# The g vector as a per-partition factor on the transposed q, and weight sums in four units

## The chip, the cores and the metric

The kernel runs on one core of a Trainium2 chip. A core has five engines that work side by side, each through its own queue in order: TensorE (PE, matrix products), VectorE (DVE), ScalarE (ACT), GpSimd (POOL) and SyncE (SP, which here only issues transfers). The metric is the time of one execution on the device in microseconds (us); the median of several runs counts.

## What is computed

Attention over 8 batches and 12 heads (448 rows, 64 columns) with root-mean-square norms on q and k, and then two matrix products with a leaky ReLU between them. Cut to what matters:

```python
def rmsnorm(x, g):
    rms = np.sqrt(np.mean(x * x, axis=-1, keepdims=True) + 1e-06)
    return x / rms * g
q_n, k_n = rmsnorm(q, g_q), rmsnorm(k, g_k)
scores = (1.0 / np.sqrt(64)) * np.matmul(q_n, k_n.transpose(0, 1, 3, 2))
attn = np.exp(scores - np.max(scores, axis=-1, keepdims=True))
attn = attn / (np.sum(attn, axis=-1, keepdims=True) + 1e-09)
o = np.matmul(attn, v)                      # (8, 12, 448, 64)
x = o.transpose(0, 2, 1, 3).reshape(3584, 768)
h = x @ w_in                                # (3584, 2048)
out = np.maximum(0.01 * h, h) @ w_out       # (3584, 768)
```

g_q, g_k and the factor 1/8 enter the scores only as the product 0.125 * g_q[d] * g_k[d] for each of the 64 columns d. The kernel applies that product to q alone.

## The kernel before

**Units.** A unit u is four heads of one batch: 24 units, three for each batch. The raw q and k of a unit lie in tiles `rq` and `rk` with 128 rows of tokens on the partitions, and 2 x 7 x 64 numbers on each. A ring of three such pairs is loaded four units ahead by SP (L107).

**Preparing a unit.** The squares `sq` are made on ACT (`prep_sq`, L130) or on POOL (`prep_sqp`, L134). DVE sums them (`ssq`, L143), ACT makes `rinv` from the sums by a logarithm and an exponential (L148, L149), and DVE multiplies raw q and raw k by it into `n16`, or n (L155, one instruction for q and one for k, 896 numbers a partition). n is then transposed into `qkT`, in which partition 64a + d holds column d of head half a. Units 0 to 5 do this on PE, with a copy out of PSUM on DVE or ACT (`prep_tr`, L163 and L164). Units 6 to 23 use a transposing DMA that SP issues (`prep_trd`, L167).

**The g product before the change.** At the start, g_q and g_k come as two rows on one partition (`grow`, L564 and L565, issued by ACT). DVE multiplies them (L573), a PE product with a column of ones spreads the row over all 128 partitions (L574), and ACT copies it to `ggb` (L578). For each unit POOL multiplies raw q in place by `ggb` (`prep_qg`, L138). This happens after the squares were taken from raw q and ahead of n.

**A unit's attention.** Scores are made in seven steps of PE (L183) into PSUM, with keys on the partitions. ACT takes their exponentials (`et`, L202), shifted by a bound that is taken from step 0: DVE reduces the scores to a maximum (`shift_max`, L220) and spreads it on a diagonal matrix dg (L222), PE multiplies it with ones (`shift_mm`, L232), DVE reduces again (L233) and forms the bias (L241). In PE's queue `shift_mm` stands behind the PV product (L324) and the column sums (`zc`, L270) of the unit before; everything later on PE stands behind it. The column sums are inverted on DVE and ACT (L287 to L293), spread by DMA (`rz`, L297), and POOL multiplies the PV result with them (`xmul_pool`, L304, writing `xt`).

**The two matrix products.** They are cut into items, in a queue. Each unit has four stages d = 0 to 3, and `fill` pops items between the attention work, in shares laid down in `WD`; after each item it runs one of the small jobs of that stage, and what is left of them at the stage's end. So the order on every engine is fixed when the program is built. Items are `moe1` (the first product, six matmuls of L345 and the leaky ReLU on ACT, L339), `moe2` (the plain second product, L385), and `seven` (the second product of two tiles by seven products of half-size blocks instead of eight, L425). `seven` needs sums of blocks of the activations (`s1`, `s2` on DVE, L406 and L409; `s3`, `s4` on POOL, L412 and L415) and four sums of blocks of `w_out` (`tw`, L400). The latter are made once, each in two halves of 1536 numbers a partition, on DVE: two sums in stage 3 of unit 5, two in stage 3 of unit 6. The first `seven` comes after the 16 `moe1` items of batch 1, which are queued in stage 3 of unit 6.

**Order in a steady unit u (u > 3).** Stage 0: scores, `shift_max`, PV and sums of u-1, `shift_mm`, exponentials; the load of u+4, `prep_qg` of u+2 and the v load of u+3 on POOL. Stage 1: `xmul_pool` of u-1, `ssq` of u+2. Stage 2: `rinv`, n and the transpose of u+2. Stage 3: weight sums, where there are any, and the squares of u+3 on ACT from unit 6 on.

Of the kernel before, what the change touches and what calls it, by code (L numbers as in the profile page):

```python
# [8 lines left out]
FP32 = mybir.dt.float32  # L9
FP16 = mybir.dt.float16  # L10
AF = mybir.ActivationFunctionType
ALU = mybir.AluOpType
# [6 lines left out]
def kernel(  # L19
# [11 lines left out]
    nc = tc.nc  # L31
# [4 lines left out]
    P = 128  # L36
# [18 lines left out]
    def aux(shape, dtype, name):  # L55
        return psum.tile(shape, dtype, tag="aux", bufs=4, name=name)
# [10 lines left out]
    nc.vector.memset(onesp, 1.0)  # L67
    eps_t = cst.tile([P, 1], FP32)
    nc.vector.memset(eps_t, 1.0e-6)
    one32 = cst.tile([1, P], FP32)  # L70
    nc.vector.memset(one32, 1.0)
    grow = cst.tile([1, 2, D], FP32)
    gate_t = cst.tile([P, 1], FP16)
    ggb = cst.tile([P, D], FP32)
    vts = [cst.tile([P, 2, NS, D], FP16, name=f"vt{i}") for i in range(NV)]
    win16 = cst.tile([P, NQ, 2, DF], FP16)
    wout16 = cst.tile([P, FT, DM], FP16)
# [42 lines left out]
    def buf(u, name):  # L120
        if name not in st[u]:
            shape, dtype, bufs = SHAPES[name]
            st[u][name] = prep_p.tile(shape, dtype, tag=name[:2] if bufs == 3 and name != "qkT" else name, bufs=bufs, name=name)
        return st[u][name]
# [8 lines left out]
        for ti in tis:  # L133
            nc.gpsimd.tensor_tensor(buf(u, f"sq{ti}"), raw[u][ti], raw[u][ti], op=ALU.mult)  # L134

    def prep_qg(u, eng, c=ALL):
        n = c[1] - c[0]
        eng.tensor_tensor(raw[u][0][:, :, c[0]:c[1]], raw[u][0][:, :, c[0]:c[1]],  # L138
                          ggb[:, None, None, :].broadcast_to([P, 2, n, D]), op=ALU.mult)

    def prep_ssq(u, c=ALL, tis=BOTH):
        for ti in tis:
# [16 lines left out]
    def prep_tr(u, ti, copies):  # L159
        tp = aux([P, NS, P], FP16, "tp")  # L160
        for (lo, hi), copy in copies:
            for x in range(lo, hi):
                nc.tensor.transpose(tp[:, x, :], buf(u, "n16")[:, ti, x].rearrange("p a d -> p (a d)"), ident16)  # L163
            copy(buf(u, "qkT")[:, ti, lo:hi], tp[:, lo:hi])  # L164

    def prep_trd(u):
        nc.sync.dma_start_transpose(  # L167
# [383 lines left out]
            job()  # L551
        flush()

    vcopy, acopy = nc.vector.tensor_copy, nc.scalar.copy
    CA, CB = (0, 4), (4, NS)
    K0, K1 = (0, 1), (1, NS)
    VV = ((ALL, vcopy),)
# [1 line left out]
    def warm(n, bank):  # L559
        for x in range(n):  # L560
            nc.tensor.matmul(bank[:, P:2 * P], onesp, onesp, start=True, stop=True)

    with tc.manual_schedule():
        nc.scalar.dma_start(grow[:, 0], g_q[None, :])  # L564
        nc.scalar.dma_start(grow[:, 1], g_k[None, :])  # L565
        nc.scalar.preload_act_table_set("natural_log_exp_and_others")
        load(0)
        load(1)
        load(2)
        gps = aux([P, 512], FP32, "gps")  # L570
        wbank = aux([P, 512], FP32, "warm")
        warm(32, wbank)
        nc.vector.scalar_tensor_tensor(grow[:, 0], grow[:, 0], 0.125, grow[:, 1], op0=ALU.mult, op1=ALU.mult)  # L573
        nc.tensor.matmul(gps[:, 0:D], one32, grow[:, 0], start=True, stop=True)  # L574
        warm(42, wbank)
        prep_sq(0, CA, (0,))
        prep_sq(0, CB, (0,))
        acopy(ggb, gps[:, 0:D])  # L578
        prep_sq(0, ALL, (1,))
        prep_qg(0, nc.gpsimd, CA)  # L580
        prep_qg(0, nc.gpsimd, CB)
        prep_ssq(0, CA, (0,))
        prep_ssq(0, CB, (0,))
        prep_rinv(0, (0,))
# [22 lines left out]
        prep_sq(2, ALL, (0,))  # L607
        load(3)
        gate(0)
        prep_qg(1, nc.gpsimd)  # L610
        prep_sqp(2, (1,))
        shift_max(0)
        shift_bank(0)
# [5 lines left out]
        def feed(u):  # L619
            load(u + 4)  # L620
            gate(u + 1)
            prep_qg(u + 2, nc.gpsimd)
            prep_sqp(u + 3)
            load_v(u + 3)

# [113 lines left out]
        for u in range(3, NU):  # L739
            for d in range(4):  # L740
# [18 lines left out]
                def job(fn, *args):  # L759
                    jobs.append(lambda: fn(*args))  # L760

                if d == 0:
                    if u == 3:
                        prep_norm(4)
                        gate(4)
                    elif narrow(u - 1):
                        job(zcol_inv, u - 1)
                    else:
                        xmul(u - 1)
                    if u + 4 < NU:  # L770
                        job(load, u + 4)
                    if u + 2 < NU:
                        prep_qg(u + 2, nc.gpsimd)
                    if u + 3 < NU:
                        load_v(u + 3)
                    if u < 6:
                        prep_sqp(u + 3)
# [4 lines left out]
                if (u, d) in ((3, 1), (4, 0)):  # L782
                    for ti in range(2):
                        prep_tr(u + 1, ti, VV)
                if u + 2 < NU:
                    if d == 1:
                        for ti in range(2):
                            job(prep_ssq, u + 2, ALL, (ti,))
                    if d == 2:
                        job(prep_rinv, u + 2)  # L790
                        for ti in range(2):
                            job(prep_norm, u + 2, ALL, (ti,))
                        if u > 3:
                            job(prep_trd, u + 2)
                if d == 3 and u in (5, 6):
                    for n in (0, 2) if u == 5 else (1, 3):
                        for x in range(2):
                            job(weight_sum, n, x)
                if d == 3 and 6 <= u < NU - 3:
                    for ti in range(2):  # L800
                        job(prep_sq, u + 3, ALL, (ti,))
# [37 lines left out]
```

## Time and profile before

| what | value |
|---|---|
| time, median of 5 runs | 444.38 us (443.87, 444.55, 444.38, 442.57, 1426.18) |
| the profiled execution | 442.99 us; its span 441.2 us |
| PE busy | 411.9 us, 93% |
| ACT busy | 309.4 us, 70% |
| DVE busy | 256.4 us, 58% |
| POOL busy | 191.4 us, 43% |
| g pass on POOL (L138), 25 times | 52.4 us, mean 2.098 us |
| xt pass on POOL (L304), 19 times | 40.1 us, mean 2.113 us |
| n on DVE (L155), 25 for q and 25 for k | 31.3 and 29.9 us |
| ssq on DVE (L143), 49 times | 50.2 us, mean 1.053 us |
| weight sums on DVE (L400), 8 times | 0.94 to 2.84 us each |
| transposing DMA (L167), 18 times | 4.1 us from issue to landing |

The span is the time from the first to the last instruction of the profiled execution; the time of an execution is a little longer. Busy shares are averages over the whole span. An engine's idle time counts only where the work that ends last stood behind it. In a listing by time each line has the start, the duration, the engine, the line of the program, the operation with output and input tiles and their shapes, and in brackets how long the engine had been idle and what released it. A group that runs back to back is one line with its count. The page also has a row for the clock that PE was granted, in tenths of full speed, over 40 equal slices of the span.

### The profile page before, as it was taken

What the parts mean: (1) busy time and instruction counts of PE and PEld (TensorE: products, weight loads), DVE (VectorE), ACT (ScalarE), POOL (GpSimd) and SP (SyncE); (2) the same over time, 40 slices, a digit from 0 to 9 for tenths busy, and PEclk for the clock granted to TensorE, in tenths of its full rate; (3) what the DMA queues carried; (4) which work ended last, traced back from release to release, by engine and by line L of the source; (5) the groups of instructions that cost most, each with busy time, mean ns of one, the idle gap of its engine ahead of it and who ended that gap; (6) DMA issues with size and microseconds to landing.
All of it is one profiled execution on the core that took longest, in us unless ns stands there. A gap on an engine that the chain in (4) does not pass through costs nothing.

```text
span 441.2 us, 8892 instructions
## 1 busy us (share of the span) xinstructions
PE 411.9 (93%) x3645; PEld 211.1 (48%) x3645; DVE 256.4 (58%) x381; ACT 309.4 (70%) x470; POOL 191.4 (43%) x132
## 2 busy tenths in 40 slices
PE   7788999677999899999999999999999999999996
PEld 7544444333344444454445444454445544555563
DVE  5897666868365954566476873386377650422062
ACT  6998977455788459977788589976987658653400
POOL 4996752604144641264255732364237601050250
PEclk9999999969799999999999999999999999999999
DMA  8999995846525597657845796748753441112004
GB/s 263 230 258 242 244 242 82 204 78 181 144 45 144 96 227 200 122 129 188 198 87 138 129 226 177 178 84 205 195 69 72 124 114 43 43 37 71 0 8 136
DMA packets 66476, 62.37 MB, mean 141 GB/s; under 512 B 35716, under 2 KB 61572, under 8 KB 66436
## 3 DMA queue, kind: packets, MB, share of 16 engines
q1 hardware_dynamic: 55840, 49.62, 43.7%
q0 software_dynamic: 10272, 11.80, 17.3%
q8 instruction: 28, 0.46, 0.4%
q10 hardware_dynamic: 324, 0.39, 0.3%
q14 instruction: 12, 0.10, 0.1%
HBM read 45.61 MB, written 11.01 MB: 128 GB/s over the span
## 4 chain that ended last, share of the span: by engine, by line
PE 69%; DVE 14%; ACT 11%; issue 5%; DVEq 0%; ACTq 0%
PE hps L345 31%; ACT et L202 7%; PE ma L425 6%; PE sT L183 6%; PE md L425 5%; PE op L385 5%; PE sT L324 4%; DVE n L155 4%; PE mc L425 3%; PE mb L425 3%; PE zc L270 2%; DVE tw L400 2%; DVE sT L220 2%; DVE ost L432 1%; DVE ssq L143 1%
## 5 line engine op out<-in xcount | busy, mean ns | idle before, releaser
L202 ACT ACTIVATE et<-sT,eb 128x896 f16<-128x896 f32 x166 | 158.6, 1005 | 16.6 <-PE sT L183 15.0
L345 PE MATMUL hps<-xt,win 128*128 128x448 f16 x756 | 153.6, 357 | 0.2 <-DVE xt L333 0.2
L345 PEld LDWEIGHTS <-win 128*128 128x128 f16 x756 | 71.4, 99 | 73.4 <-issue 13.2
L304 POOL TENSOR_TENSOR xt<-x,rz 128x896 f16<-128x896 f32 x19 | 40.1, 2113 | 131.8 <-DMA rz<-zs 109.1
L339 ACT ACTIVATE gt<-hps 128x448 f16<-128x448 f32 x126 | 66.0, 541 | 22.1 <-PE hps L345 21.4
L138 POOL TENSOR_TENSOR rq<-rq,ggb 128x896 f32<-128x896 f32 (+2 forms) x25 | 52.4, 2098 | 41.7 <-ACT sq L130 28.5
L155 DVE TENSOR_TENSOR n<-rq,rinv 128x896 f16<-128x896 f32 (+2 forms) x25 | 31.3, 1255 | 59.9 <-issue 42.3
L183 PE MATMUL sT<-qkT 64*64 64x448 f16 x664 | 52.2, 363 | 5.4 <-ACT et L202 4.7
L282 ACT COPY x<-sT 128x896 f32<-128x896 f32 x19 | 17.2, 906 | 50.8 <-DVE sT L233 48.1
L143 DVE TENSOR_REDUCE ssq<-sq 128x14 f32<-128x896 f32 (+2 forms) x49 | 50.2, 1053 | 1.0 <-ACT sq L130 1.0
L425 PEld LDWEIGHTS <-sa 128*128 128x128 f16 x352 | 32.8, 98 | 26.3 <-issue 6.1
L412 POOL TENSOR_TENSOR sa<-gt 128x512 f16<-128x512 f16 (+1 forms) x15 | 25.8, 1721 | 28.4 <-ACT gt L339 24.5
L385 PE MATMUL op<-wout,gt 128*128 128x384 f16 x192 | 36.3, 341 | 0.0
L425 PEld LDWEIGHTS <-gt 128*128 128x128 f16 x264 | 25.2, 98 | 20.6 <-issue 4.6
L220 DVE TENSOR_REDUCE sT<-sT 128x1 f32<-128x896 f32 x22 | 24.0, 1092 | 18.8 <-PE sT L183 18.8
L183 PEld LDWEIGHTS <-qkT 64*64 64x64 f16 x672 | 15.8, 104 | 39.5 <-issue 35.5
L415 POOL TENSOR_TENSOR sa<-gt,sa 128x512 f16<-128x512 f16 (+1 forms) x15 | 26.7, 1777 | 15.1 <-DVE sa L409 10.5
L425 PE MATMUL ma<-wout,gt 128*128 128x384 f16 x176 | 32.3, 326 | 0.1
L155 DVE TENSOR_TENSOR n<-rk,rinv 128x896 f16<-128x896 f32 (+2 forms) x25 | 29.9, 1198 | 0.0
L324 PE MATMUL sT<-et,vt 64*64 64x448 f16 x532 | 28.5, 349 | 0.3
L406 DVE TENSOR_TENSOR sa<-gt 128x512 f16<-128x512 f16 (+1 forms) x15 | 10.7, 710 | 30.3 <-ACT gt L339 30.3
L385 PEld LDWEIGHTS <-gt 128*128 128x128 f16 x192 | 18.4, 102 | 15.5 <-issue 5.7
(86 smaller groups left out, 454.4 us busy)
## 6 DMA issues: line engine op xcount, KB each, us to landing
rq<-in_q_dram SPq DMA_DIRECT2D x24, 448.0 KB, 5.0
rk<-in_k_dram SPq DMA_DIRECT2D x24, 448.0 KB, 6.1
out_dram<-ost SPq DMA_DIRECT2D x52, 192.0 KB, 3.5
rz<-zs SPq DMA_DIRECT2D x38, 224.0 KB, 3.2
vt<-in_v_dram POOLq DMA_DIRECT2D x24, 224.0 KB, 4.4
win<-in_moe_w_in_dram POOLq DMA_DIRECT2D x8, 384.0 KB, 12.2
wout<-in_moe_w_out_dram POOLq DMA_DIRECT2D x2, 1536.0 KB, 28.6
out_dram<-ost SPq DMA_DIRECT2D x4, 96.0 KB, 2.1
```

The costliest lines, as they stand in the source:

```text
L138: eng.tensor_tensor(raw[u][0][:, :, c[0]:c[1]], raw[u][0][:, :, c[0]:c[1]], ggb[:, None, None, :].broadcast_to([P, 2, n, D]), op=ALU.mult)
L143: nc.vector.tensor_reduce(buf(u, "ssq")[:, ti, :, c[0]:c[1]], buf(u, f"sq{ti}")[:, :, c[0]:c[1]], axis=AXL.X, op=ALU.add)
L155: nc.vector.tensor_tensor(buf(u, "n16")[:, ti, c[0]:c[1]].rearrange("p s a d -> p a s d"), src[:, :, c[0]:c[1]], buf(u, "rinv")[:, ti, :, ...
L183: nc.tensor.matmul(banks[a][64 * r:64 * r + 64, 0:S].rearrange("p (t x) -> p t x", t=NS), kT(u, r, a, t), qT(u, r, a), start=True, stop=True)
L202: nc.scalar.activation(s["et"][:, t], sT[:, :, 0:S], AF.Exp, bias=s["eb"], scale=1.0)
L220: nc.vector.tensor_reduce(s["spare"][:, 511:512], sT[:, :, 0:S], axis=AXL.XY, op=ALU.max)
L304: nc.gpsimd.tensor_tensor(xts[b][:, g], s["x32"], s["rz"], op=ALU.mult)
L324: nc.tensor.matmul(s["pv"][r][64 * a:64 * a + 64, 0:S], vts[u % NV][64 * r:64 * r + 64, a, t], s["et"][64 * r:64 * r + 64, t, a], start=(t ...
L339: nc.scalar.activation(dst, src, AF.Prelu, bias=0.0, scale=1.0, alpha=0.01)
L345: nc.tensor.matmul(hps[:, 0:S], win16[:, kt // 2, kt % 2, ts(ft, P)], xt[:, kt // 2, kt % 2], start=(kt == 0), stop=(kt == KT - 1))
L385: nc.tensor.matmul(op2[:, 0:HC], gt[:, ft, ds(col(t), P)], wout16[:, ft, ds(HC * half, HC)], start=(ft == 0), stop=(ft == FT - 1))
L425: nc.tensor.matmul(bank[:, 0:HC], a[:, f], b[:, f], start=(first and f == 0), stop=(f == HF - 1), skip_group_check=not first)
```

## The change

POOL's pass over raw q is gone for all units. The vectors g_q and g_k are loaded with their 64 numbers on 64 partitions, twice (partitions 0 to 63 and 64 to 127), g_q by two DMAs of ACT and g_k by two of POOL. One DVE instruction makes `gcol` = 0.125 * g_q * g_k, one number on each partition. The q half of `qkT` is multiplied by it: in units 0 to 5 inside the copy out of PSUM (on DVE a multiplication in place of a copy, on ACT a copy with a scale), in units 6 to 23 by a DVE instruction of its own, in place on `qkT`, in stage 1 of the unit before (`prep_g`). The row product on PE, its PSUM bank and ACT's copy fall away, and the 74 warming products of PE at the start become 75 in one piece. The weight sums come in stage 3 of units 4, 5, 6 and 7, one sum (two halves) in each, instead of two sums in unit 5 and two in unit 6. The order of the four sums is now 0, 1, 2, 3; it was 0, 2, 1, 3.

```diff
@@ -67,11 +67,9 @@
     nc.vector.memset(onesp, 1.0)
     eps_t = cst.tile([P, 1], FP32)
     nc.vector.memset(eps_t, 1.0e-6)
-    one32 = cst.tile([1, P], FP32)
-    nc.vector.memset(one32, 1.0)
-    grow = cst.tile([1, 2, D], FP32)
+    gpair = cst.tile([P, 2], FP32)
+    gcol = cst.tile([P, 1], FP32)
     gate_t = cst.tile([P, 1], FP16)
-    ggb = cst.tile([P, D], FP32)
     vts = [cst.tile([P, 2, NS, D], FP16, name=f"vt{i}") for i in range(NV)]
     win16 = cst.tile([P, NQ, 2, DF], FP16)
     wout16 = cst.tile([P, FT, DM], FP16)
@@ -133,10 +131,8 @@
         for ti in tis:
             nc.gpsimd.tensor_tensor(buf(u, f"sq{ti}"), raw[u][ti], raw[u][ti], op=ALU.mult)
 
-    def prep_qg(u, eng, c=ALL):
-        n = c[1] - c[0]
-        eng.tensor_tensor(raw[u][0][:, :, c[0]:c[1]], raw[u][0][:, :, c[0]:c[1]],
-                          ggb[:, None, None, :].broadcast_to([P, 2, n, D]), op=ALU.mult)
+    def prep_g(u):
+        nc.vector.tensor_scalar(buf(u, "qkT")[:, 0], buf(u, "qkT")[:, 0], gcol, None, op0=ALU.mult)
 
     def prep_ssq(u, c=ALL, tis=BOTH):
         for ti in tis:
@@ -161,7 +157,7 @@
         for (lo, hi), copy in copies:
             for x in range(lo, hi):
                 nc.tensor.transpose(tp[:, x, :], buf(u, "n16")[:, ti, x].rearrange("p a d -> p (a d)"), ident16)
-            copy(buf(u, "qkT")[:, ti, lo:hi], tp[:, lo:hi])
+            copy(buf(u, "qkT")[:, ti, lo:hi], tp[:, lo:hi], ti == 0)
 
     def prep_trd(u):
         nc.sync.dma_start_transpose(
@@ -551,7 +547,18 @@
             job()
         flush()
 
-    vcopy, acopy = nc.vector.tensor_copy, nc.scalar.copy
+    def vcopy(dst, src, scaled=False):
+        if scaled:
+            nc.vector.tensor_scalar(dst, src, gcol, None, op0=ALU.mult)
+        else:
+            nc.vector.tensor_copy(dst, src)
+
+    def acopy(dst, src, scaled=False):
+        if scaled:
+            nc.scalar.activation(dst, src, AF.Copy, bias=0.0, scale=gcol)
+        else:
+            nc.scalar.copy(dst, src)
+
     CA, CB = (0, 4), (4, NS)
     K0, K1 = (0, 1), (1, NS)
     VV = ((ALL, vcopy),)
@@ -561,24 +568,19 @@
             nc.tensor.matmul(bank[:, P:2 * P], onesp, onesp, start=True, stop=True)
 
     with tc.manual_schedule():
-        nc.scalar.dma_start(grow[:, 0], g_q[None, :])
-        nc.scalar.dma_start(grow[:, 1], g_k[None, :])
+        for a in range(2):
+            nc.scalar.dma_start(gpair[64 * a:64 * a + 64, 0:1], g_q[:, None])
+            nc.gpsimd.dma_start(gpair[64 * a:64 * a + 64, 1:2], g_k[:, None])
         nc.scalar.preload_act_table_set("natural_log_exp_and_others")
         load(0)
         load(1)
         load(2)
-        gps = aux([P, 512], FP32, "gps")
         wbank = aux([P, 512], FP32, "warm")
-        warm(32, wbank)
-        nc.vector.scalar_tensor_tensor(grow[:, 0], grow[:, 0], 0.125, grow[:, 1], op0=ALU.mult, op1=ALU.mult)
-        nc.tensor.matmul(gps[:, 0:D], one32, grow[:, 0], start=True, stop=True)
-        warm(42, wbank)
+        warm(75, wbank)
+        nc.vector.scalar_tensor_tensor(gcol, gpair[:, 0:1], 0.125, gpair[:, 1:2], op0=ALU.mult, op1=ALU.mult)
         prep_sq(0, CA, (0,))
         prep_sq(0, CB, (0,))
-        acopy(ggb, gps[:, 0:D])
         prep_sq(0, ALL, (1,))
-        prep_qg(0, nc.gpsimd, CA)
-        prep_qg(0, nc.gpsimd, CB)
         prep_ssq(0, CA, (0,))
         prep_ssq(0, CB, (0,))
         prep_rinv(0, (0,))
@@ -607,7 +609,6 @@
         prep_sq(2, ALL, (0,))
         load(3)
         gate(0)
-        prep_qg(1, nc.gpsimd)
         prep_sqp(2, (1,))
         shift_max(0)
         shift_bank(0)
@@ -619,7 +620,6 @@
         def feed(u):
             load(u + 4)
             gate(u + 1)
-            prep_qg(u + 2, nc.gpsimd)
             prep_sqp(u + 3)
             load_v(u + 3)
 
@@ -769,8 +769,6 @@
                         xmul(u - 1)
                     if u + 4 < NU:
                         job(load, u + 4)
-                    if u + 2 < NU:
-                        prep_qg(u + 2, nc.gpsimd)
                     if u + 3 < NU:
                         load_v(u + 3)
                     if u < 6:
@@ -782,6 +780,8 @@
                 if (u, d) in ((3, 1), (4, 0)):
                     for ti in range(2):
                         prep_tr(u + 1, ti, VV)
+                if d == 1 and 5 <= u < NU - 1:
+                    job(prep_g, u + 1)
                 if u + 2 < NU:
                     if d == 1:
                         for ti in range(2):
@@ -792,10 +792,9 @@
                             job(prep_norm, u + 2, ALL, (ti,))
                         if u > 3:
                             job(prep_trd, u + 2)
-                if d == 3 and u in (5, 6):
-                    for n in (0, 2) if u == 5 else (1, 3):
-                        for x in range(2):
-                            job(weight_sum, n, x)
+                if d == 3 and 4 <= u < 8:
+                    for x in range(2):
+                        job(weight_sum, u - 4, x)
                 if d == 3 and 6 <= u < NU - 3:
                     for ti in range(2):
                         job(prep_sq, u + 3, ALL, (ti,))
```

## The prediction

> **What bounds the kernel now.** I read the page first (engine shares, clock row, chain), then the list of TensorE's waits, then the timeline of the stretches where those waits lie, and last the clock in slices of 1 us there. TensorE (PE) is busy 412 of 441 us, and the chain of waits is 69% PE. ACT has the second highest share (309 us), but over 164 to 180 us PE is busy 16.0 of 16.0 us with ACT at 14.3. So a change pays only where PE stands still, or runs slowly. The page's clock row and chain, and PE's waits:
>
> ```profile
> PEclk9999999969799999999999999999999999999999
> PE 69%; DVE 14%; ACT 11%; issue 5%; DVEq 0%; ACTq 0%
> ...
> PE sT L232 <- DVE dg L222: 12.7, 5, 6.1
> ```
>
> The clock row has two dips, slices 8 and 10 (88 to 99 and 110 to 121 us). The wait line says that in five places PE stood for 12.7 us in all, 6.1 in the longest, for the small matrix dg that VectorE (DVE) makes when a unit's score maximum is known. PE's timeline gives the three that count; the bracket is the idle time ahead of the instruction:
>
> ```profile
> 91.10 0.27 PE L232 MATMUL sT<-dg,onesp 128*128 128x64 f16 x2 [6.07 <-DVE dg L222]
> ...
> 110.82 0.26 PE L232 MATMUL sT<-dg,onesp 128*128 128x64 f16 x2 [3.78 <-DVE dg L222]
> ...
> 148.00 0.22 PE L232 MATMUL sT<-dg,onesp 128*128 128x64 f16 x2 [2.16 <-DVE dg L222]
> ```
>
> Why is dg late? The timeline of DVE and GpSimd (POOL) ahead of the first (start, duration, engine, line):
>
> ```profile
> 79.91 1.08 DVE L155 TENSOR_TENSOR n<-rq,rinv 128x896 f16<-128x896 f32 x1
> 80.16 2.77 POOL L304 TENSOR_TENSOR xt<-x,rz 128x896 f16<-128x896 f32 x1 [1.69 <-DMA rz<-zs]
> 80.91 2.97 DVE L155 TENSOR_TENSOR n<-rk,rinv 128x896 f16<-128x896 f32 x1
> ...
> 82.89 2.94 POOL L138 TENSOR_TENSOR rq<-rq,ggb 128x896 f32<-128x896 f32 x1
> 83.81 2.83 DVE L400 TENSOR_TENSOR tw<-wout 128x1536 f16<-128x1536 f16 x1
> ...
> 86.57 0.54 DVE L389 COPY ost<-op 128x384 f32<-128x384 f32 x1
> 87.03 2.68 DVE L400 TENSOR_TENSOR tw<-wout 128x1536 f16<-128x1536 f16 x3
> 89.64 1.09 DVE L220 TENSOR_REDUCE sT<-sT 128x1 f32<-128x896 f32 x1
> ```
>
> PE finished unit 5's PV and column sums at 85.03 and stood. DVE had to do n, then four weight sums, then the maximum (L220). The first sum took 2.83 us, the next three 0.89 each: it began while POOL ran the g pass (L138), and ended 0.8 us after it (82.89 + 2.94 = 85.83). The n ahead was held in the same way by POOL's xt.
>
> Ahead of 110.82 it is the same: four sums from 104.00, one of them 2.83 us under the g pass of 106.12. Ahead of 148.00 no sum runs, but L406 (0.69 us elsewhere) took 2.21 under the g pass of 143.51. The stall also has a second price, shown by the clock in slices (columns: PE, PE loads, DVE, ACT, POOL busy, then clock):
>
> ```profile
> 88.00:89.00 1.00, 0.00 (x0) 0.00 (x0) 1.00 (x2) 0.00 (x0) 0.00 (x0) 0.94 0.77 98
> 89.00:90.00 1.00, 0.00 (x0) 0.00 (x0) 1.00 (x2) 0.00 (x0) 0.00 (x0) 0.50 0.72 114
> ...
> 94.00:95.00 1.00, 1.00 (x5) 0.44 (x4) 0.00 (x0) 0.64 (x2) 0.00 (x0) 0.50 0.00 0
> 95.00:96.00 1.00, 1.00 (x5) 0.43 (x3) 0.00 (x0) 0.00 (x0) 0.00 (x0) 0.64 0.03 7
> 96.00:97.00 1.00, 1.00 (x13) 0.42 (x12) 0.79 (x2) 0.47 (x1) 0.00 (x0) 1.00 0.92 197
> ```
>
> The clock is halved from about 89 to 95.6, so that 16 matmuls of L385 take 4.80 us there against 2.71 later. After 110.82, 18 of L345 take 5.99 against 3.51.
>
> **What the Trainium skill says.** "SBUF — State Buffer", section "SBUF: two separate sides": VectorE with two SBUF inputs (or in a two-port mode) and GpSimd share a port pair under an exclusive lock, held for a whole instruction. The trace agrees: 2.83 against 0.89 us. "TensorE: Matmul & The Clock Gate", Part 1: the clock halves after a mostly idle window of about 3.4 us, and the window runs freely. Here it fell 3.9 us after PE stopped at 85.03 and 2.6 after it stopped at 107.04, and not in the stall of 2.16. "VectorE: DVE Perf Modes", the perf-mode tier table: a fp16 tensor_scalar in SBUF runs at four elements a cycle, from PSUM at two at most, like a copy. The trace has no such instruction; its PSUM copy (L164, 0.61 us for 896) fits the two. "DMA: Bandwidth & Descriptors", Anatomy of one DMA: a POOL-issued DMA has some 2.0 us fixed. The g loads here, issued by ACT, took about 2.6 us (end of issue 1.53, DVE's use at 4.16).
>
> **The change part by part.** DVE's hand-over is 1.46 us from the start of L220 to PE's L232 (89.64 to 91.10). "Boundary u" is that of unit u.
>
> *g passes removed.* 25 on POOL, 52.4 us, none itself on PE's path except through the lock. At boundary 9, L406 falls from 2.21 to 0.69: 1.5 us gained, all of it inside a stall of 2.16. POOL's next work there, a v load and the L412 pass, must wait for PE's PV first, so that it shouldn't move into the gap. POOL's earlier squares and loads in the first 44 us free nobody on the chain: n follows DVE's own work or ACT's rinv there.
>
> *Weight sums spread.* Eight pieces of 0.9 us, two at each of boundaries 5 to 8, instead of four at 6 and 7.
> - Boundary 5 (new): DVE was free at 70.21 (0.17 us ahead of L220). 70.21 + 1.8 + 1.46 = 73.5 against PE's 72.29: 1.2 us lost.
> - Boundary 6: sums start at 83.81, no g pass: 0.9 + 0.47 (the ost copy) + 0.9 + 1.46 gives 87.54 against 91.10. Gain 3.56; a stall of 2.5 remains (from 85.03), since xt still holds n.
> - Boundary 7: 104.00 + 1.8 + 1.46 = 107.26 against 110.82. Gain 3.56; 0.2 remains.
> - Boundary 8 (new): L409 ended at 126.73; + 1.8 + 1.46 = 130.0 against 129.19: 0.8 lost. But L415 on POOL (1.15 us) comes free at that moment; as at 80.9, where xt got in between two DVE passes, it will likely hold the second sum. I take 1.9; the ends are 0.8 and 3.0 (held twice).
> - Clock: 5.99 − 3.51 = 2.48 back after boundary 7, surely, since 0.2 us of stall can't halve it. After boundary 6, 4.80 − 2.71 = 2.09 back if 2.5 us of stall keep the clock. That lies between the 2.16 that kept it and the 2.64 that didn't; I take it as kept. The other end is 0.
>
> *g as a factor of qkT.* Units 6 to 23: 18 tensor_scalar on DVE. By the skill's breakdown (150 + 8 + 224 cycles at 0.96 GHz) an estimate of 0.40 us each, 1.1 at one element a cycle. They wait for a transpose issued a unit earlier, landed after 4.1 us, so nothing stands behind them. They lie ahead of the ssq, after which DVE is idle (6.2 us ahead of 174.86; still 2.5 us at 157 in a unit with the seven products). Cost 0 at both ends; without that gap 7.2 us in all. Units 0 to 5: the factor is in the PSUM copies. DVE's at 0.61 as before: 0. At one element a cycle each would take 0.44 more, three of them on the chain of the first 44 us: +1.3.
>
> *Start.* Out: the g row product, its matmul and copy on ACT (0.4 us between the squares), two g passes (2.23 us). n of the second q chunk waited for them. In: four loads of 64 single numbers, two on POOL behind its mask work (1.31), and a product on DVE queued ahead of the first ssq, for which ACT's rinv, n and all of unit 0 wait. Two POOL issues at 0.77 each end at 2.85; 2.0 to 2.6 us later the product runs, at 4.9 to 5.5 instead of 4.16. The first ssq, 4.70 before, starts at 5.1 to 5.7. Reduction of k then ends at 7.3 to 7.9 against 7.59. Gain 0.2, from −1.0 to +0.7.
>
> **Sum.** −1.2 + 3.56 + 3.56 + 2.48 + 2.09 − 1.9 + 1.5 + 0.2 = 10.3 us. The profiled execution took 442.99 us (span 441.2): 432.7. The median of the runs shown is 444.38, 1.4 above it: 434.1 is the forecast.
>
> **The rivals.**
> 1. *The clock still halves at boundary 6* (the window falls badly). Gain 8.2: 436.2. For: 2.64 us sufficed once. Against: 2.16 didn't. 0.25.
> 2. *More falls away*: boundary 8 at 0.8, the start at its best: 12 us, 432.4 and less. 0.12.
> 3. *A new late one eats half*: g lands at 8 us or PSUM copies run at one element a cycle, and something behind boundary 7 comes late (xt is done 9.9 us after L232, its matmuls due at about 9.9 once warm). 438 to 443. 0.04.
> 4. *Slower: four stalls for two.* Place: boundaries 5 to 8. If every piece meets a POOL pass (2.83 each, 3.9 more per boundary), the stalls are 5.1, 6.4, 4.1 and 4.7, each with a cold clock at about 2.3: 29.5 us against today's 6.07 + 3.78 + 2.09 + 2.48 = 14.4. Less 1.7 for boundary 9 and the start, +13.4: 457.8. It decides from about 4 us a boundary with its cold stretch. For: xt, L412 and L415 stay on POOL. Against: the pass that held the sums was the g pass each time, and around 70 and 104 POOL would be empty. 0.08 with all else that ends above.
> 5. *No change* within 0.3% (1.3 us, about what can be told apart here): 0.03.
>
> **How the numbers follow.** Forecast 0.48. Faster: 0.48 + 0.25 + 0.12 + 0.04 = 0.89; same 0.03; slower 0.08. The range 430 to 440 takes in both clock cases, both ends of boundary 8 and of the start, and the slower copies; outside are 4, 5 and the tails of 2 and 3, some 0.15.
>
> **What would show it.** Right: PE's wait for L222 falls from 12.7 to about 7 us; no stall over 3 us; the clock row without its second dip; sums at 0.9 us each; L406 never at 2.2. Wrong: sums of 2.8 us, dips at four places, a first ssq after 6 us, or tensor_scalar rows above 1.1 us.

## The result, and the profile after

The changed kernel takes 442.74 us (median of 44 executions) against 443.80 (79 executions of the kernel before): ratio 0.9967, interval 0.9953 to 0.9981. It is faster, by about 1 us or 0.2 to 0.5%. The forecast was 10 us, and 442.74 lies outside its range of 430 to 440.

The executions of the changed kernel do not lie around one value: 17 lie from 438.9 to 440.5 us, nine from 442.6 to 443.2 and 16 from 444.1 to 444.8. The other two, of 528 and 1352 us, stand apart, and as the one of 1352 us (mean matmul of L341 937 ns instead of 353) was the one profiled, the profile below is of the same kernel in run r1. That execution took 439.96 us and belongs to the first group.

Of its page, the span, the clock row, the chain by engine, and of PE's waits the two longest:

```profile
span 438.1 us, 8869 instructions
...
PEclk9698999989999999999999999999999999999999
...
PE 63%; ACT 17%; DVE 13%; issue 4%; DMA 2%; POOL 0%; DVEq 0%; POOLq 0%; ACTq 0%
...
PE sT L228 <- DVE dg L218: 6.9, 7, 2.5
PE tp L159 <- DVE n L151: 4.7, 1, 4.7
```

The wait for dg fell from 12.7 to 6.9 us, and no single stall is above 2.5 us. But a transfer has come onto the chain (DMA 2%), there is a new wait of 4.7 us for n, and the clock row has dips near its start. The code has moved by some lines: in the changed kernel `shift_mm` is L228, the weight sums are L396, s1 is L402, s3 and s4 are L408 and L411, xt is L300 and n is L151; runs with added lines differ by a few more. PE's timeline shows the boundaries of units 5, 6, 8 and 9 (boundary u is where PE waits for dg of unit u):

```profile
78.92 0.22 PE L228 MATMUL sT<-dg,onesp 128*128 128x64 f16 x2 [0.92 <-DVE dg L218]
94.08 0.22 PE L228 MATMUL sT<-dg,onesp 128*128 128x64 f16 x2 [2.44 <-DVE dg L218]
127.88 0.22 PE L228 MATMUL sT<-dg,onesp 128*128 128x64 f16 x2 [2.46 <-DVE dg L218]
145.31 0.22 PE L228 MATMUL sT<-dg,onesp 128*128 128x64 f16 x2 [0.47 <-DVE dg L218]
```

The forecast had 1.2, 2.5, 1.9 (ends 0.8 and 3.0) and 0.7 here. So the boundaries are about where they were expected, except unit 8, which lies above the 1.9 of the sum. The start is not. Its timeline, over all engines:

```profile
0.74 1.20 ACTq L572 DMA_DIRECT2D gpair<-in_g_q_dram  x2
...
2.34 0.55 POOL L573 DMA_DIRECT2D gpair<-in_g_k_dram  x1
...
2.89 1.48 POOL L108 DMA_DIRECT2D vt<-in_v_dram  x2
...
7.90 0.95 ACT L128 ACTIVATE sq<-rk 128x896 f32<-128x896 f32 x1 [2.65 <-DMA rk<-in_k_dram]
9.84 0.16 DVE L580 SCALAR_TENSOR_TENSOR gcol<-gpair 128x1 f32<-128x1 f32 x1 [8.49 <-DMA gpair<-in_g_k_dram]
9.91 2.13 DVE L139 TENSOR_REDUCE ssq<-sq 128x8 f32<-128x512 f32 x3
...
12.70 0.40 PE L159 MATMUL tp<-ident,n 128*128 128x128 f16 x4 [4.72 <-DVE n L151]
```

DVE stood 8.5 us for g, and the first ssq behind it in its queue started at 9.91 us; before it was 4.70. One column was enough to hold the engine that everything at the start goes through. After PE had stood, its clock was halved, from 13.2 to 20.0 us, and again from 33.7 to 37.1; in the kernel before it was whole until 88.9.

The table splits the spans at the same instructions of PE: the first wait of the first matrix product for DVE's xt ("first product"), `shift_mm` at boundaries 5, 6 and 8, and the first wait of an md product (one of the products of `seven`) for DVE, at 160.82 us before.

| stretch, us | before | changed (r1, 439.96 us) | r6, 444.60 us | r12 |
|---|---|---|---|---|
| start to first product | 43.47 | 49.12 | 48.80 | 44.05 |
| to boundary 5 | 28.82 | 29.80 | 29.81 | 29.81 |
| to boundary 6 | 18.81 | 15.16 | 15.16 | 15.16 |
| to boundary 8 | 38.09 | 33.80 | 33.54 | 33.53 |
| to the md product | 31.63 | 30.18 | 35.35 | 30.33 |
| to the end | 280.38 | 280.04 | 280.14 | 279.92 |
| span | 441.2 | 438.1 | 442.8 | 432.8 |

r6 is the changed kernel with two v loads issued later, which leaves everything after the start as it was. Its profiled execution took 444.60 us, and shows where such executions lose 5 us: in one stretch, from boundary 8 to the md product.

### The profile page after: what moved, and what is told of

It is laid out like the page before. It is cut to its first block, busy times and chain, and to the rows that moved or that the text cites. A ratio compares the mean times of both kernels' runs of the same rounds, so it can differ in the third digit from the quotient of the medians.

```text
span 1349.9 us, 8869 instructions
## 1 busy us (share of the span) xinstructions
PE 1343.1 (99%) x3644; PEld 435.2 (32%) x3644; DVE 255.1 (19%) x398; ACT 325.7 (24%) x469; POOL 137.4 (10%) x109
## 4 chain that ended last, share of the span: by engine, by line
PE 99%; ACT 0%; DVE 0%; issue 0%
PE hps L341 38%; PE sT L179 9%; PE op L381 8%; PE ma L421 7%; PE md L421 7%; PE mc L421 7%; PE sT L320 7%; PE mb L421 4%; PE zc L266 3%; PE pv L320 2%; PE warm L568 2%; PE sT L249 1%; PE tp L159 1%; PE pb L568 1%; PE sT L348 1%; PE zt L249 0%
## 5 line engine op out<-in xcount | busy, mean ns | idle before, releaser
L341 PE MATMUL hps<-xt,win 128*128 128x448 f16 x756 | 514.7, 937 | 0.0
L341 PEld LDWEIGHTS <-win 128*128 128x128 f16 x756 | 147.7, 200 | 341.8 <-issue 341.8
L179 PE MATMUL sT<-qkT 64*64 64x448 f16 x664 | 128.4, 842 | 0.5 <-ACT qkT L558 0.5
L381 PE MATMUL op<-wout,gt 128*128 128x384 f16 x192 | 114.9, 848 | 0.0
L421 PE MATMUL ma<-wout,gt 128*128 128x384 f16 x176 | 104.7, 831 | 0.0
L320 PE MATMUL sT<-et,vt 64*64 64x448 f16 x532 | 102.1, 988 | 0.0
L151 DVE TENSOR_TENSOR n<-rq,rinv 128x896 f16<-128x896 f32 (+2 forms) x25 | 28.1, 1125 | 225.7 <-ACT rinv L145 212.3
L320 PEld LDWEIGHTS <-vt 64*64 64x64 f16 x672 | 51.8, 212 | 52.9 <-issue 52.8
L300 POOL TENSOR_TENSOR xt<-x,rz 128x896 f16<-128x896 f32 x19 | 39.3, 2066 | 247.8 <-DMA rz<-zs 235.7
L421 PE MATMUL md<-tw,sa 128*128 128x384 f16 x88 | 53.1, 839 | 0.0
L421 PE MATMUL mb<-tw,sa 128*128 128x384 f16 x88 | 52.9, 839 | 0.0
L421 PE MATMUL md<-tw,gt 128*128 128x384 f16 x88 | 52.9, 843 | 0.0
```

The lines of the kernel that those rows point to most:

```text
L151: nc.vector.tensor_tensor(buf(u, "n16")[:, ti, c[0]:c[1]].rearrange("p s a d -> p a s d"), src[:, :, c[0]:c[1]], buf(u, "rinv")[:, ti, :, ...
L179: nc.tensor.matmul(banks[a][64 * r:64 * r + 64, 0:S].rearrange("p (t x) -> p t x", t=NS), kT(u, r, a, t), qT(u, r, a), start=True, stop=True)
L300: nc.gpsimd.tensor_tensor(xts[b][:, g], s["x32"], s["rz"], op=ALU.mult)
L320: nc.tensor.matmul(s["pv"][r][64 * a:64 * a + 64, 0:S], vts[u % NV][64 * r:64 * r + 64, a, t], s["et"][64 * r:64 * r + 64, t, a], start=(t ...
L341: nc.tensor.matmul(hps[:, 0:S], win16[:, kt // 2, kt % 2, ts(ft, P)], xt[:, kt // 2, kt % 2], start=(kt == 0), stop=(kt == KT - 1))
L381: nc.tensor.matmul(op2[:, 0:HC], gt[:, ft, ds(col(t), P)], wout16[:, ft, ds(HC * half, HC)], start=(ft == 0), stop=(ft == FT - 1))
```

## The experiments

Each edit is against the kernel named with it. Ratios are to the kernel before on the same chip, with 95% intervals.

**r1: the changed kernel again.**

> The changed kernel as it is, for a profile of an ordinary execution; the one shown is of an execution of 1350 us in which each matmul took almost three times as long, so only its start and its DVE and POOL rows can be read. Theory A (late g): the product of g_q and g_k on DVE waits until about 10 us for the loads of single numbers, the first ssq starts at about 10.2 us instead of 4.7, and unit 0 is 4 to 5.5 us late; the boundaries gain as forecast, 8 to 10 us, so the time is 438 to 441. Theory B (nothing lost at the start, boundaries gain little): first ssq before 6 us, PE's wait for dg still above 10 us.

443.61 us in 20 executions (439.06 to 445.07), ratio 0.9983 (0.9956 to 1.0011). Theory A is right for the start and for the profiled execution. But 14 of the 20 executions lie above its 441, so it lacked something; and over these 20 alone the gain isn't clear of noise.

**r2: the sums alone.** Kernel before, with

```diff
-                if d == 3 and u in (5, 6):
-                    for n in (0, 2) if u == 5 else (1, 3):
-                        for x in range(2):
-                            job(weight_sum, n, x)
+                if d == 3 and 4 <= u < 8:
+                    for x in range(2):
+                        job(weight_sum, u - 4, x)
```

> The kernel before with its weight sums spread over units 4 to 7; the g passes stay on POOL and the start is as before. Theory A: the start is not hurt, boundaries 6 and 7 gain, less than with the g passes gone, since those still hold sums: 4 to 8 us faster than before, 436 to 440. Theory B: within 1 us of before.

438.71 us, ratio 0.9889 (0.9863 to 0.9915): five us faster. This half of the change, alone, does more than the whole. Theory A is right. The stalls are 4.34 us at boundary 6, 0.16 at 7 and 2.32 at 8. At boundary 6 a g pass still held a sum (one of 2.83 us).

**r3: the g part alone.** The changed kernel with the same lines put back.

> The changed kernel with the weight sums put back as two in unit 5 and two in unit 6. Theory A: start 4 to 5.5 us later; the sums no longer meet a g pass, which gives 2 us at each of boundaries 6 and 7, and 1.5 at boundary 9: 444 to 446, slower by up to 2 us. Theory B: 440 to 443.

441.06 us, ratio 0.9937 (0.9916 to 0.9958). Faster, within theory B's range, where theory A had said slower by up to 2 us. Its start was late as expected (first product at 48.48 us). The stalls at boundaries 6 and 7 are 4.18 and 1.90 us instead of 6.07 and 3.78, 1.9 us each, as theory A had it. What it left out is that the halved clock behind them got shorter too, 3.4 us each time instead of 6.8. All eight sums ran free of the lock. PE's two waits, and the group of the weight sums (shortest, median and longest in ns):

```profile
94.21 0.22 PE L228 MATMUL sT<-dg,onesp 128*128 128x64 f16 x2 [4.18 <-DVE dg L218]
111.48 0.22 PE L228 MATMUL sT<-dg,onesp 128*128 128x64 f16 x2 [1.90 <-DVE dg L218]
...
L396 DVE TENSOR_TENSOR tw<-wout x4: 941/944/944, 88.8 to 91.9; 128x1536 f16<-128x1536 f16 x4
L396 DVE TENSOR_TENSOR tw<-wout,tw x4: 948/954/955, 106.5 to 109.1; 128x1536 f16<-128x1536 f16 x4
```

**r4: g as rows again.** Changed kernel, with

```diff
-            nc.scalar.dma_start(gpair[64 * a:64 * a + 64, 0:1], g_q[:, None])
-            nc.gpsimd.dma_start(gpair[64 * a:64 * a + 64, 1:2], g_k[:, None])
+        nc.scalar.dma_start(grow[:, 0], g_q[None, :])
+        nc.scalar.dma_start(grow[:, 1], g_k[None, :])
...
-        nc.vector.scalar_tensor_tensor(gcol, gpair[:, 0:1], 0.125, gpair[:, 1:2], op0=ALU.mult, op1=ALU.mult)
+        for a in range(2):
+            nc.vector.scalar_tensor_tensor(gdup[:, a], grow[:, 0], 0.125, grow[:, 1], op0=ALU.mult, op1=ALU.mult)
+        nc.tensor.matmul(gps[:, 0:1], gdup.rearrange("p a d -> p (a d)"), one32, start=True, stop=True)
...
+        acopy(gcol, gps[:, 0:1])
```

> The changed kernel with g_q and g_k loaded as two rows of 64 numbers by ACT, as in the kernel before, multiplied on DVE, turned into the column by a PE product and copied by ACT; all else as changed. Theory A: first ssq back at 4.7 to 5.2 us, 4 to 5.5 us faster than the changed kernel on this chip: 435 to 438. Theory B: same as the changed kernel within 1 us.

440.84 us (437.19 to 442.63), ratio 0.9918 (0.9890 to 0.9945), some 2.8 us under r1 and so between the two theories. The first ssq is back at 4.69 us, but the mark of the first product is at 46.06 and not at 43.5: half of the loss stayed. ACT's timeline shows where:

```profile
10.46 0.95 ACT L131 ACTIVATE sq<-rq 128x896 f32<-128x896 f32 x1 [2.42 <-DMA rq<-in_q_dram]
11.31 0.67 ACT L561 ACTIVATE qkT<-tp,gcol 128x512 f16<-128x512 f16 x1
```

The squares of unit 1 stand ahead of the copy of unit 0's qkT in ACT's queue, and waited for raw q of unit 1. A cause that suggests itself, tested in r5: the v loads of units 0 and 1, queued on POOL behind the g passes until then (issued at 7.87 us), were now issued at 1.27 and 2.49 us, among the raw loads.

**r5: r4 with the v loads later.** The two calls moved:

```diff
-        load_v(0)
-        load_v(1)
...
         gate(0)
+        load_v(0)
+        load_v(1)
```

> The row start of r4, and the v loads of units 0 and 1 put behind the first small POOL copy (L240 in the changed kernel) that waits for n of unit 0. Theory A2 (two causes at the start: the late product of g, and v loads that came forward when the g passes left POOL and now compete with raw q and k): ACT's squares of unit 1 start before 8.2 us instead of 10.46, the first score before 10.5 us instead of 13.03, some 2.5 us less than r4: 434 to 438. Theory A1 (the late product alone): as r4 within 1 us.

The squares start at 7.96 us and the first score at 10.54, as theory A2 had it: there are two causes at the start. 439.89 us (434.77, 439.68, 440.10, 440.30), ratio 0.9880 (0.9819 to 0.9941): the start is mended, but only one of the four executions, 434.77, lies in the expected range; the others are 5 us above that one.

**r6: the changed kernel with the v loads later** (the same two calls moved).

> The changed kernel with its loads of single numbers, and only the v loads put later as in r5. If the single numbers are slow by themselves, the product on DVE still starts at 8 us or later; if the v loads make them late, it starts before 6 us. Theory A2: between the two, at 6 to 8 us, and 2 to 4 us faster than the changed kernel: 438 to 441. Theory A1: still near 9.8, time as the changed kernel.

The product of g still starts at 9.8 us, so my 6 to 8 was wrong and theory A1 right: the v loads do not make g late. Beside the raw loads, loads of 64 single numbers took 3.8 to 7.4 us from issue to landing. In the changed kernel the early v loads therefore cost little, 0.3 us at the first product (49.12 against 48.80): DVE waits for g anyway. 441.67 us (439.15 to 445.30), ratio 0.9959 (0.9923 to 0.9994).

**r7: the product of g later in DVE's queue.** Changed kernel; the line moved from ahead of the first `prep_ssq` to behind the four `prep_norm` calls of unit 0. The transposes of unit 0's q, whose copy needs g, were moved behind it, which leaves PE's and ACT's order as it was.

> The changed kernel with only the product of g moved in DVE's queue, from ahead of the first ssq to behind n of unit 0; loads as changed. Theory A2: first ssq at 4.8 us instead of 9.9, but the squares of rk and of unit 1 wait for their loads, and the copy with the factor waits until about 10 to 11.5: first score at 12.5 to 13.5 instead of 15.24, 2 us faster than the changed kernel. Theory A1: the whole 5 us come back, first score before 11.

First ssq at 4.94 us, first score at 12.38 instead of 15.24: a little better than expected. 437.58 us (436.16 to 441.76), ratio 0.9886 (0.9827 to 0.9945). So about 3 us of the loss came from the place of one instruction in a queue, and not from the late load as such. The loads still cost something: the squares of unit 0's k waited 0.94 us for raw k (before they did not wait).

r6 and r7, in which the instructions after the start stand in the same order, together show what happens in an execution near 444 us. From boundary 8 on, first r6 (444.60 us), PE and then DVE and POOL:

```profile
127.31 0.27 PE L228 MATMUL sT<-dg,onesp 128*128 128x64 f16 x2 [2.49 <-DVE dg L218]
127.39 5.21 PE L341 MATMUL hps<-xt,win 128*128 128x448 f16 x18
...
139.61 0.82 PE L421 MATMUL mb<-tw,sa 128*128 128x384 f16 x4 [1.57 <-DVE sa L405]
141.06 2.72 PE L421 MATMUL ma<-wout,gt 128*128 128x384 f16 x8 [0.63 <-DVE ost L437]
...
136.10 2.16 DVE L402 TENSOR_TENSOR sa<-gt 128x512 f16<-128x512 f16 x1 [5.33 <-ACT gt L335]
138.30 1.25 DVE L405 TENSOR_TENSOR sa<-sa,gt 128x512 f16<-128x512 f16 x1
...
135.90 2.08 POOL L300 TENSOR_TENSOR xt<-x,rz 128x896 f16<-128x896 f32 x1 [10.08 <-DMA rz<-zs]
```

and the same work in r7 (436.16 us):

```profile
124.11 0.22 PE L228 MATMUL sT<-dg,onesp 128*128 128x64 f16 x2 [2.48 <-DVE dg L218]
124.17 3.57 PE L341 MATMUL hps<-xt,win 128*128 128x448 f16 x18
...
131.59 0.42 DVE L402 TENSOR_TENSOR sa<-gt 128x512 f16<-128x512 f16 x1 [4.06 <-ACT gt L335]
132.04 0.42 DVE L405 TENSOR_TENSOR sa<-sa,gt 128x512 f16<-128x512 f16 x1
...
132.49 2.08 POOL L300 TENSOR_TENSOR xt<-x,rz 128x896 f16<-128x896 f32 x1 [9.86 <-DMA rz<-zs]
```

The stall at boundary 8 is the same, 2.5 us. In r6 the clock was halved at its end, and 18 matmuls took 5.21 us instead of 3.57. Therefore the activations (gt) came late, and L402 (s1), which sums them, started 0.2 us after POOL's xt instead of 0.9 us before it. It was held for 2.16 us, PE waited for the sum behind it, and the clock was halved a second time (r6 in slices of 1 us; the clock is the third number from the end):

```profile
127.00:128.00 1.00, 0.69 (x4) 0.36 (x4) 0.61 (x3) 0.00 (x0) 0.00 (x0) 0.66 0.85 124
128.00:129.00 1.00, 1.00 (x4) 0.42 (x3) 0.93 (x3) 1.00 (x2) 0.00 (x0) 0.50 0.58 91
...
130.00:131.00 1.00, 1.00 (x5) 0.46 (x4) 0.77 (x1) 0.97 (x3) 0.00 (x0) 0.63 0.00 0
...
140.00:141.00 1.00, 0.43 (x3) 0.14 (x2) 1.00 (x2) 0.39 (x2) 0.84 (x1) 0.99 0.00 0
...
142.00:143.00 1.00, 1.00 (x5) 0.50 (x4) 1.00 (x2) 0.00 (x0) 0.00 (x0) 0.50 0.00 0
143.00:144.00 1.00, 1.00 (x7) 0.28 (x9) 0.67 (x1) 0.18 (x1) 0.00 (x0) 0.50 0.00 0
144.00:145.00 1.00, 1.00 (x11) 0.31 (x4) 0.00 (x0) 0.94 (x2) 0.00 (x0) 0.81 0.03 4
```

The other profiles of kernels with a weight sum at boundary 8 and without g passes fit this. In r5 (440.10 us) and r10 (445.20 us) the clock is halved after boundary 8, s1 takes 2.21 and 2.35 us, and PE waits 1.61 and 1.75 us for the sum behind it. In r1, r4, r9 and r12 the clock is not halved there, and s1 takes 0.42 or 0.43 us.

Why does an equal stall go both ways? The slices tell when the clock changed. A mean of 0.66 in slice 127 means that it was whole for 0.32 us and halved for 0.68, so it fell at 127.32. In the same way it rose at 130.74, fell at 140.98 and rose at 144.38: distances of 3.42, 10.24 and 3.40 us, one, three and one times 3.41. In the profile before, the four changes lie at 88.88, 95.72, 109.36 and 116.20, two, four and two times 3.41 apart, and so it is, to 0.03 us, with all changes of every profile that has several. Within one execution they lie on a grid of 3.41 us, and the grid lies differently in each execution. In r6 the stall of boundary 8 (124.82 to 127.31) lies inside one step of that grid, 123.90 to 127.32, in which PE was busy for 0.93 us; then the clock fell. The equal stall of boundary 6 (91.33 to 93.77) is cut by a step at 93.18. PE was busy for 1.56 us in the step that ends there, and the clock stayed whole. Between 40 and 400 us, over all profiles whose grid can be read, each of the 12 steps with the clock whole and PE busy for less than 39% was followed by a halved clock, none of those above 45% was, and between the two it went both ways. Before 40 us, where PE's products are of other shapes, two steps of 54 and 59% (r9 and r1) were followed by a halved clock too, so the busy share is only a rough measure.

**r9: the stalls filled.** Changed kernel, in `shift_mm`:

```diff
             pb = st[u - 1]["pslot"][:, :, S:S + 64]
+            if u in (6, 8):
+                for x in range(30):
+                    nc.tensor.matmul(pb[:, x % 2], onesp, onesp[:, 0:64], start=True, stop=True)
```

> The changed kernel with 30 small products of ones on PE, into free columns of the PV bank, ahead of the wait for dg at boundaries 6 and 8; they change no result. Theory C (cold clock and its follow-up): the stalls stay at 2.4 to 2.5 us but filled, the clock isn't halved after boundaries 6 and 8, so L402 (s1) doesn't meet POOL's xt and no wait of mb for s2 arises: the executions near 444.4 vanish, nearly all lie at 437 to 439.5. Theory D (the times near 444 have another origin): executions on both sides of 442 as before.

439.77 us, all six executions within 439.15 to 440.92, ratio 0.9922 (0.9899 to 0.9945). The values near 444 are gone; s1 (0.42 us) meets no pass, and the clock is whole from 39 us to the end. The times lie where the first group of the changed kernel lies, about 1.5 us above what was expected. In the profile the start is later than in r1 (boundary 5 at 79.80 us against 78.92), and the whole clock after boundary 6 gains little, since boundary 7 then stalls for 1.31 us. Of the changed kernel's own executions 25 of 42 lie above 442 us, so that six of six below it are hardly chance (an estimate: 17/42 to the sixth power, 0.4%). With r6 and r7 this shows the cause of the times near 444: the halved clock after boundary 8. Filling boundary 8 alone was not tried.

**r10: all four loads of g by ACT.** Changed kernel; `nc.gpsimd` to `nc.scalar` in the loads of g_k.

> The changed kernel with all four loads of single numbers issued by ACT, none by POOL. If POOL's queue makes them late, the product on DVE starts before 6.5 us and 3 us or more come back; if loads of 64 single numbers are slow beside the raw q and k loads, it starts at 8 us or later, as with the changed kernel (9.8), and the time is within 1.5 us of it.

The product starts at 10.6 us, and the median is 445.17 (440.12 to 445.67), ratio 1.0018 (0.9988 to 1.0049). So it isn't POOL's queue. The edit also let the v loads come forward to 1.27 and 2.49 us, but r6 has shown that they do not make g late. That leaves the single numbers, beside the raw loads; whether the count of 64 pieces or their landing on 64 partitions is what costs, and what they would take without the raw loads, was not tried.

**r8 and r11: the sums where DVE is idle.** r8 is r5, and r11 the kernel before, with the sums' lines of stage 3 taken out and, behind the `prep_ssq` jobs of stage 1,

```diff
+                        for n in {4: (0,), 7: (1, 2, 3)}.get(u, ()):
+                            for x in range(2):
+                                job(weight_sum, n, x)
```

> r5 with the weight sums in stage 1, where DVE waits for rinv: one sum in unit 4, three in unit 7 (DVE idle 5.2 and 8.4 us there in the kernel before). If the boundaries are set by what stands ahead of the maximum on DVE, the stalls of 0.9, 2.4 and 2.5 us at boundaries 5, 6 and 8 fall to 0, 0.6 and 0.4, and the clock is not halved there: 4 to 7 us faster than r5, 429 to 433. If something else ends the boundaries, within 1.5 us of r5.

> The kernel before (g passes on POOL, start as before) with only the weight sums moved to stage 1, one in unit 4 and three in unit 7, as in r8. What it lacks against r8 is the g change. If the boundaries were late by the sums alone, 428 to 431, like r8; if the g passes still hold n, s1 or sums, 432 to 435.

r8: 429.26 us, ratio 0.9665 (0.9634 to 0.9695). r11: 430.27 us, ratio 0.9704 (0.9676 to 0.9732). So the move of the sums alone, with the g passes left on POOL, brings nearly all of it. Against r11, r8 gains at boundary 9, where the g pass held s1 (a stall of 2.16 us in r11 and 0.55 in r8), and loses about as much at its start (boundary 5 at 73.52 us against 72.11). In r8's DVE timeline six half sums fill the gap ahead of n, and PE's longest wait for dg is 0.7 us:

```profile
105.85 1.82 DVE L399 TENSOR_TENSOR tw<-wout,tw 128x1536 f16<-128x1536 f16 x2
107.58 1.82 DVE L399 TENSOR_TENSOR tw<-wout 128x1536 f16<-128x1536 f16 x2
109.32 1.82 DVE L399 TENSOR_TENSOR tw<-wout,tw 128x1536 f16<-128x1536 f16 x2
111.06 1.08 DVE L154 TENSOR_TENSOR n<-rq,rinv 128x896 f16<-128x896 f32 x1
...
134.60 0.22 PE L231 MATMUL sT<-dg,onesp 128*128 128x64 f16 x2 [0.55 <-DVE dg L221]
...
PE sT L231 <- DVE dg L221: 2.5, 6, 0.7
```

**r12: both losses taken away.** r5 with the edit of r9.

> r5 (g as rows, v loads later) with the filling products of r9 at boundaries 6 and 8: the change with both of its losses taken away, and the boundaries otherwise as changed. Theory: the start (5.5 us) and the halved clock with its follow-up (up to 5.2 us) are all that the forecast of 434.1 lacked: 433.5 to 436 in nearly all executions, none above 438. Rival: something else is lost too, 437 or more, or executions on both sides of 437 still.

435.64 us (435.07 to 436.85), ratio 0.9826 (0.9805 to 0.9847), all in one group, as the theory had it. The span of its profile is 8.4 us under the one before, against the 10.3 of the sum.

## Why the prediction was wrong

Two steps failed: the start, which the sum had at +0.2 us and which measured −5.65, and what follows boundary 8, for which the sum had nothing and which took some 5 us in the executions near 444. A third term, from boundary 6 to 8, came out 1.7 us too large.

*What bounds the kernel*: right. The boundaries were late by DVE, and the two prices, stall and cold clock, were the ones to count. r11, which moves the sums and nothing else, is 13.0 us faster than the kernel before, and r8 14.4.

*g passes removed*: right where it was counted. Without a g pass the sums of r3 take 0.94 to 0.96 us each, and boundary 9 fell from 2.16 to 0.47 us. But I wrote that POOL's earlier squares and loads "free nobody on the chain", and did not ask whom they would disturb. The v loads of units 0 and 1 came forward by some 5 us into the raw loads. In the changed kernel the wait for g hides most of this (r6 against r1: 0.3 us); once g is early it costs 2.5 us at the first score (13.03 in r4 against 10.54 in r5).

*Start*: the step that failed most. The prediction had two POOL issues "end at 2.85; 2.0 to 2.6 us later the product runs, at 4.9 to 5.5". It ran at 9.84. I took the latency of a row of 64 numbers for that of 64 single numbers: the row was in use 2.6 us after the end of its issue, the last of the singles 6.95 us after (2.89 to 9.84). The 2.0 us at the lower end is the fixed cost that the prediction cites; these loads took 3.8 to 7.4 us from issue to landing in r1, so it did not hold for them. The term was +0.2 with its worst end at −1.0, and measured −5.65 in r1 (49.12 against 43.47) and −5.33 in r6. The halved clock at 13 and 34 us, which the term does not have either, lies in the same stretch; its share was not measured apart. The prediction did name what stood behind the product, and a first ssq after 6 us as a sign of being wrong, which came. Rival 3 had g landing at 8 us and 438 to 443, at 0.04; the measured time lies in its range, but its second half, xt late behind boundary 7, did not come. With the start alone mis-sized the forecast would have been 440.0, at the edge of its range.

*Boundaries 5 and 6*: right. 1.0 lost (1.2 said), 3.65 gained (3.56 said).

*Boundary 7 and the clock after 6*: over-counted. In r12 the clock was whole to the end, and boundaries 6 to 8 took 33.5 us against 38.1. The sum had 3.56 + 2.48 + 2.09 − 1.9 = 6.2 there, and 4.6 came. When PE runs warm after boundary 6, POOL's xt meets n at boundary 7, as it met it at boundary 6. r7 shows it, DVE and then POOL:

```profile
98.25 1.08 DVE L151 TENSOR_TENSOR n<-rq,rinv 128x896 f16<-128x896 f32 x1
99.25 2.97 DVE L151 TENSOR_TENSOR n<-rk,rinv 128x896 f16<-128x896 f32 x1
...
98.51 2.77 POOL L300 TENSOR_TENSOR xt<-x,rz 128x896 f16<-128x896 f32 x1 [10.06 <-DMA rz<-zs]
```

Boundary 7 then stalls 1.31 us and not the 0.2 of the sum. With a cold stretch (a halved clock) after boundary 6, as in r1, it stalls for 0.19 us only; so the whole clock was worth 0.3 us there, not 2.09 (33.80 against r12's 33.53).

*Boundary 8*: 2.46 instead of 1.9, between the sum's value and its end of 3.0, through the meeting that was foreseen, with s4 on POOL (L411 in r1, DVE and then POOL):

```profile
123.70 2.79 DVE L396 TENSOR_TENSOR tw<-wout,tw 128x1536 f16<-128x1536 f16 x2
...
123.93 1.74 POOL L411 TENSOR_TENSOR sa<-gt,sa 128x512 f16<-128x512 f16 x1 [1.89 <-DVE sa L405]
```

The new loss is what follows. I asked whether the stall of 2.5 us at boundary 6 would halve the clock, and never asked it of boundary 8, where it decides: there the cold stretch makes L402 meet xt, and 5.2 us go (35.35 against 30.18). The sum has nothing for this, and it is the second step that failed. The Trainium skill ("TensorE: Matmul & The Clock Gate", Part 1) says that the window by which PE's activity is judged runs freely, from which it follows that an equal stall can fall either way. The runs agree: the same 2.5 us is followed by a halved clock in r6 and by a whole one in r7, and the changes of the clock lie on a grid of 3.41 us whose position differs from execution to execution. Where that page has the clock fall after an idle window, the runs decide: PE was busy for up to 38% of the steps behind which it always fell. So the prediction asked the wrong question when it weighed 2.5 us between "the 2.16 that kept it and the 2.64 that didn't". The second number was misread too: the mean of 0.68 in slice 109 puts the fall at 109.36, 2.3 us after PE stopped at 107.04. And the stall of 2.16 (145.84 to 148.00) was cut by a step of the grid at 146.91. Rival 4 had stalls and cold clocks at the new boundaries, but not what a cold stretch makes collide behind one of them.

*g as a factor of qkT*: right. The median is 0.434 us in the gap (0.40 estimated; the longest of the 18 took 1.48), and from PSUM 0.68 us against 0.61.

Together: r12 keeps 8.4 of the forecast's 10.3. In the changed kernel the start takes 5.65 us (r1), and the event at boundary 8 some 5 us more in the executions near 444, which are 16 of the 42. No execution of the unedited changed kernel from that group was profiled; r6, whose order after the start is the same, stands for it. What makes the nine near 442.7 us was not profiled either and stays open. The sum put at boundary 8 was not tried alone: r3, without it, has no stall there and eight executions from 439.26 to 442.13 us; r2, with it and with the g passes, stalls for 2.32 us and has four executions within 1.6 us.

## What to carry to other kernels

A pass taken off an engine brings everything queued behind it forward: ask of each freed transfer what it will run into. Do not put an instruction that waits for a load ahead of the work of the engine that everything goes through, and do not price a load of single numbers by a row of the same bytes. A gap found idle in the trace is a better home for one-time work than an even spread over boundaries that are already late, and where a stall may halve the clock, as those of 2.5 us did here, count it twice: once for itself, and once for what the slower stretch makes collide.

## What the runs showed of the hardware

- Four loads of 64 numbers of 4 bytes each onto 64 partitions, beside the raw loads of the start, landed 3.8 to 7.9 us after their issue (r1, r9, r10), by ACT's and POOL's queues or by ACT's alone; two rows of the same 64 numbers were in use 2.6 us after the end of their issue (r4: 1.50 to 4.07 us).
- One kernel, with all its instructions in the same order, had executions 5 us apart. Stalls of 2.44 to 2.51 us were followed by a halved clock of 3.4 us in r1, r4, r5, r6 and r10, and by a whole one at other boundaries of r1, r4, r6 and r10 and in r7. In each of the eleven profiles in which the clock changed, all its changes lie whole multiples of 3.41 us apart; between 40 and 400 us, where PE was busy for less than 39% of one such step, the clock was halved behind it, all 12 times. Thirty small products into a stall of 2.5 us, 1.05 us in all, went with a whole clock at both boundaries in both profiles (r9, r12).
- DVE and POOL held each other by their order of start, to a fraction of a us: L402 took 0.42 us when it started 0.9 us ahead of xt (r7), and 2.16 when it started 0.2 us behind it (r6); xt took 2.77 us instead of 2.08 where it began while the first n pass was still running (r7).
